# A spectral mixer fused with a SoLU feed-forward block: quarter products gathered behind each pair's seventh product on a new plan, and the exponentials' sum taken to the deviations

## The chip, the core and the metric

The kernel runs on one core of a Trainium2 chip. The metric is device time in microseconds, the median of several executions. Five engines work side by side, each through its own queue in order: TensorE (PE, with its weight loads PEld), VectorE (DVE), ScalarE (ACT), GpSimd (POOL), and SyncE (SP), which only issues DMAs. ACT and POOL issue DMAs too.

## The reference, cut to what matters

```python
# x: 8 entries of 3136 rows x 256 channels
X = np.fft.rfft(x, axis=1)
y = np.fft.irfft(X * (filt_r + 1j * filt_i)[None], n=3136, axis=1)
h = y.reshape(25088, 256) @ w_in                       # 256 x 1024
e = np.exp(h - h.max(-1, keepdims=True))
solu = h * e / (e.sum(-1, keepdims=True) + 1e-9)
mu, var = solu.mean(-1, keepdims=True), solu.var(-1, keepdims=True)
out = ((solu - mu) / np.sqrt(var + 1e-6) * g_ln) @ w_out   # 1024 x 256
```

All of it is float32.

## The kernel before, in words

**Two streams in one queue.** The 25088 rows are 196 blocks of 128, taken in 98 pairs. `step(k)` issues what belongs to block k; even and odd steps of one pair (j = k // 2) differ. Beside this main stream runs the Fourier mixing of the entries still to come: entry 0 and part of entry 1 come first, alone, and entries 2 to 7 are cut into small jobs that are laid between the main stream's products. All is issued in an order written out by hand (`manual_schedule`), so each engine's queue holds its instructions in the order of `step`.

**Main stream of a pair.** The expansion of a pair is a 2x2 by 2x2 block product done with seven products instead of eight (`product(j, m)`, 128x512 each, two instructions): 1, 2, 6, 7 in the even step, 5, 3, 4 in the odd one. Sums of inputs are made by POOL (`pair_sums`). Two PSUM banks take them (`ps_m`); ACT copies bank 0 out (`keep`), DVE adds and takes the running minimum (`finish`). Two blocks later ACT does the exponential with its sum (`exponential`), DVE multiplies (`normalize`, with the sum's inverse as its scalar, made by two DVE instructions on 128x1), a block later DVE transposes 32x32 squares (`turn`), ACT squares for the variance (`square`), and SP regroups the transposed rows by DMA (`regroup`). Once for four blocks POOL makes the deviations (`deviations`) and one small matmul turns them (`regroup_deviations`). The projection is seven products again (`project(p, m)`, 8 instructions of 128x128 each) for a pair p four or five behind: 5, 3, 4 in the even step, 1, 2, 6, 7 in the odd one, in two banks of `ps_o` (bank 0: 1, 6, 5, 3; bank 1: 2, 7, 4). POOL makes the sums (`project_sums`), ACT scales bank 0 out (`keep_out`), DVE scales and adds bank 1 (`finish_out`). Product 4 adds onto bank 1, so it follows the `finish_out(p, 1, 1, ...)` that reads the bank after product 7; the next product 2 starts bank 1 afresh, behind `finish_out(p, 1, 0, ...)`.

**Quarter products.** A job of entries 2 to 7 uses TensorE as four 64x64 arrays. There are four kinds, named by their PSUM tiles:

- `pa`, `first_quarters`: eight in an entry, each after a POOL sum and a DVE difference of the rows; two ACT copies follow, and a store by POOL.
- `pb`, `forward`: seven in an entry; DVE multiplies its result by the filter in two parts of three instructions (`multiply`, `pr` and `pi`).
- `pc`, `inverse`: after both parts; two ACT copies and a store of g follow.
- `py`, `back_halves` with `join_halves`: eight in an entry; one ACT copy and two DVE instructions follow.

`PLAN` gives, for each entry, the steps of the eight `pa`, the seven `pb` and the eight `py`. Lists by step (`early`, `middle`, `late`, `first_parts`, `second_parts`, `loads`, ...) hold the jobs as closures, and `step` empties them at fixed places. PSUM: `ps_t` has two banks in turn (`pa`, `py`), `ps_b` two (`pb`, `pc`), `ps_m` two, `ps_o` two: eight in all.

For an entry from 2 on with a spectrum job at step t, before: `forward` in `early[t]` (middle of an even step), part 0 of `multiply` near the end of the same step, part 1 in the middle of step t + 1, `inverse` at its end. Odd steps open with the finish of product 5, `finish_out(p, 0, 0, ...)`, part 1, `turn`, two `finish`, `normalize` on DVE. A `pa` stands at the end of its step, an odd one for entries 3 to 7; a `py` in the middle of an even one.

Of the kernel before, what the change touches and what calls it, by code (L numbers as in the profile page):

```python
# [17 lines left out]
P = 128  # L18
B, S, C = 8, 3136, 256
DFF = 1024  # L20
# [19 lines left out]
    ([5, 7, 8, 9, 10, 11, 12, 13], range(18, 32, 2), [34, 36, 38, 40, 42, 44, 46, 46]),  # L40
    ([15, 23, 25, 27, 29, 31, 33, 35], range(38, 52, 2), range(54, 70, 2)),
    (range(39, 55, 2), range(58, 72, 2), range(76, 92, 2)),
    (range(63, 79, 2), range(82, 96, 2), range(100, 116, 2)),
    (range(87, 103, 2), range(106, 120, 2), range(126, 142, 2)),
    (range(111, 127, 2), range(130, 144, 2), range(150, 166, 2)),
]
EPS_LN, EPS_SM = 1e-6, 1e-9

# [46 lines left out]
def kernel(  # L95
# [48 lines left out]
    nc.vector.memset(neg_half, -0.5)  # L144

# [45 lines left out]
    class Spectrum:  # L191
# [5 lines left out]
        def __init__(self, e, pools, load, load_de):  # L197
            self.e, self.pools = e, pools
            self.load, self.load_de = load, load_de
            self.spare = {}  # L200
            self.units = [(i, min(2, NP - i)) for i in range(0, NP, 2)]
            self.xs, self.t1s, self.t2s, self.fs, self.prods, self.gs, self.des, self.spectra, self.diffs = (
                {} for _ in range(9))
# [52 lines left out]
        def difference(self, i):  # L256
            rows = slice(0, 64 + N1)
            xi = self.xs[i]
            self.diffs[i] = diff = self.pools["diff"].tile([P, 2, C], FP32, name=f"diff_{self.e}_{i}",
                                                           tag="diff")  # L260
            nc.vector.tensor_tensor(out=diff[rows], in0=xi[rows, 2:4, :], in1=xi[rows, 0:2, :],
                                    op=ALU.subtract)
# [7 lines left out]
        def first_quarters(self, i, pss):  # L270

            xi, diff = self.xs[i], self.diffs.pop(i)
            for j, rhs in enumerate((xi[:, 0:2, :], diff)):
                for g in range(2):
                    rows = (64, NK // 2)[j]
                    nc.tensor.matmul(out=pss[g][64 * j:64 * j + rows],
                                     lhsT=wq_t[64 * g:64 * g + N1, j, 0:rows],
                                     rhs=rhs[64 * g:64 * g + N1], start=True, stop=True)
            rows = slice(0, 64 + NK // 2)
            for g in range(2):  # L280
                nc.scalar.copy(out=xi[rows, 2 * g:2 * g + 2, :], in_=pss[g][rows])
# [359 lines left out]
    def psum_pair(name, other):  # L641
# [11 lines left out]
             for name, bufs in (("r", 4), ("diff", 1), ("t2", 1), ("p", 1), ("g", 1))}  # L653
# [26 lines left out]
    def prepare_w_out(step):  # L680
# [3 lines left out]
        if step == 0:  # L684
# [3 lines left out]
            for i, h, _ in quarters:  # L688
                for f in range(KF // 2):
                    fg = KF // 2 * h + f  # L690
                    nc.vector.tensor_scalar(out=w_out_sb[:, i, f], in0=w_out_sb[:, i, f],
                                            scalar1=g_sb[:, fg:fg + 1], scalar2=-float(DFF),
# [27 lines left out]
    sums, ms, hs, nmaxs, es, solus, squares = {}, {}, {}, {}, {}, {}, {}  # L720
# [61 lines left out]
    def exponential(k):  # L782

        e = wk.tile([P, DFF], FP32, name="e", tag="e")
        esum = small.tile([P, 1], FP32, name="esum", tag="esum", bufs=2)
        nc.scalar.activation(out=e, in_=hs[k], func=AFT.Exp, bias=nmaxs.pop(k)[:, 1:2], scale=-1.0,  # L786
                             accum_out=esum)
        es[k] = e, esum

    def normalize(k):  # L790

        g, i = divmod(k, 4)
        if i == 0:
            variances[g] = small.tile([P, 4], FP32, name=f"var_{g}", tag="var")
        e, esum = es.pop(k)
        rsum = small.tile([P, 1], FP32, name="rsum", tag="rsum", bufs=2)
        nc.vector.tensor_scalar(out=rsum, in0=esum, scalar1=EPS_SM, scalar2=float(DFF), op0=ALU.add,
                                op1=ALU.mult)
        nc.vector.reciprocal(out=rsum, in_=rsum)
        solus[k] = solu = hs.pop(k)  # L800
        nmu = small.tile([P, 1], FP32, name="nmu", tag="nmu", bufs=2)
        nc.vector.scalar_tensor_tensor(out=solu, in0=e, scalar=rsum, in1=solu, op0=ALU.mult,  # L802
# [3 lines left out]
    def square(k):  # L806
# [4 lines left out]
                             accum_out=variances[g][:, i:i + 1])  # L811

# [23 lines left out]

    def deviations(g):
        rs = small.tile([P, 4], FP32, name=f"rs_{g}", tag="rs", bufs=2)
        nc.gpsimd.tensor_scalar(out=rs, in0=variances.pop(g), scalar1=1.0 / DFF, scalar2=EPS_LN,
                                op0=ALU.mult, op1=ALU.add)  # L840
# [67 lines left out]
    def store_out(p):  # L908
# [13 lines left out]
     spectrum_loads) = ([[] for _ in range(blocks + LAG + 1)] for _ in range(11))  # L922

    def ahead(t, by):
        return loads[max(0, t - by)]
# [3 lines left out]
    for e in range(1, B):  # L929
# [5 lines left out]
        for i, t in enumerate(first_at):  # L935
# [10 lines left out]
            else:  # L946

                row_loads.append((t, t - 2, -1, lambda sp=sp, i=i: sp.fetch_quarters(i, nc.sync.dma_start)))
                differences[t].append(lambda sp=sp, i=i: sp.difference(i))
                products[t].append(lambda sp=sp, i=i: sp.sum(i))  # L950
                late[t].append(lambda sp=sp, i=i: sp.first_quarters(
                    i, [psum(f"pa_{sp.e}_{i}_{g}") for g in range(2)]))
                stores[t + 1].append(lambda sp=sp, i=i, dma=dma: sp.store_quarters(i, dma))
        for i, t in enumerate(spectrum_at):
# [5 lines left out]
            fetches = ahead(t, 2) if e == 1 and t < 8 else spectrum_loads[t - 2]  # L960
            fetches.append(lambda sp=sp, i=i, dma=dma: sp.fetch(i, dma))
            ahead(t, 1 if e == 1 and i % 2 == 1 else 2).append(lambda sp=sp, i=i: sp.fetch_filter(i))
            fetches.append(lambda sp=sp, i=i: sp.fetch_de(i))
            early[t].append(lambda sp=sp, i=i, o=other: sp.forward(i, psum_pair(f"pb_{sp.e}_{i}", o)))
# [9 lines left out]
        for ch, t in enumerate(back_at):  # L974
            row_loads.append((
                t, t - 1, spectrum_at[-1] + 2, lambda e=e, ch=ch: fetch_back(e, ch)))
# [16 lines left out]

    def step(k):
# [5 lines left out]
        sums_of_x = differences[k] + products[k]  # L1000
# [22 lines left out]
        if not odd:  # L1023
# [35 lines left out]
            for job in spectrum_loads[k]:  # L1059
                job()  # L1060
# [23 lines left out]
            for job in second_parts[k] + middle[k] + first_parts[k]:  # L1084
                job()
            if proj and p not in last:
                finish_out(p, 1, 0, (1, 0), 1)
                store_out(p)
        else:
# [77 lines left out]
```

## Time and profile before

| | |
|---|---|
| median of 3 runs | 1602.72 us (1601.0 to 1605.67) |
| profiled execution, span from first to last instruction | 1598.0 us |
| mean granted TensorE clock in it | 0.997 |
| PE / DVE / ACT / POOL busy | 1548.0 / 1310.2 / 915.8 / 1177.0 us |
| idle before ACT L901, ended by PE | 244.6 us |
| HBM read, written | 124.51 MB, 81.40 MB |

The span is the profiled execution's own time; what lies around it is not seen in the profile. Pair 9 begins at 245.1 us, pair 97 at 1546.0 us. A line `L754` is `product`, `L885` is `project`, `L308` a `forward` or `inverse`, `L276` `first_quarters`, `L381` `back_halves`, `L802` `normalize`, `L818` `turn`, `L775` and `L778` `finish`, `L905` `finish_out`, `L329` to `L331` `multiply`, `L261` `difference`. In a timeline the first two columns are the start and the time of a run of like instructions, both in us; in the table of groups the figures are count, busy us, mean ns of one, and idle us of the engine before them.

### The profile page before, as it was taken

The numbers are of one execution on the slowest core, as the hardware profiler recorded it, in microseconds if no ns is written. First come the engines' busy times: TensorE is split into PE (matmuls) and PEld (weight loads), VectorE is DVE, ScalarE is ACT, GpSimd is POOL, SyncE is SP. The second block draws the span as 40 slices with busy tenths as digits, with TensorE's granted clock in tenths as the row PEclk, the third lists the DMA queues.
The fourth block names the chain that finished last, engine by engine and source line by source line (L and its number), as shares of the span: only waits on it lengthen the run. The fifth ranks groups of instructions, "written<-read, shape, count | busy, mean of one in ns | idle before, by whom it ended". The sixth has DMA issues, their size and how long they took to land. (4 is left out here: it accounts for less than half of the span.)

```text
span 1598.0 us, 37061 instructions
## 1 busy us (share of the span) xinstructions
PE 1548.0 (97%) x12828; PEld 1055.5 (66%) x12828; DVE 1310.2 (82%) x2639; ACT 915.8 (57%) x1825; POOL 1177.0 (74%) x1371
## 2 busy tenths in 40 slices
PE   5998999999999999999999999999999999999997
PEld 1463567666666676667766776667776777777777
DVE  1887888998998889888988889987898777777773
ACT  2245655656565656565566656665555666665653
POOL 4555986688768867886778877886866867677775
PEclk8999999999999999999999999999999999999999
DMA  9989978776987588766886678766784544343434
GB/s 261 288 272 261 262 214 236 215 228 175 247 245 231 157 230 238 230 177 169 235 240 195 166 196 256 209 183 174 222 220 127 134 125 127 96 113 99 113 103 115
DMA packets 343804, 311.14 MB, mean 195 GB/s; under 512 B 27835, under 2 KB 310100, under 8 KB 343620
## 3 DMA queue, kind: packets, MB, share of 16 engines
q1 hardware_dynamic: 271476, 170.45, 40.4%
q0 software_dynamic: 33744, 98.81, 20.6%
q10 hardware_dynamic: 38400, 39.53, 8.2%
q8 instruction: 104, 1.70, 0.5%
q14 instruction: 80, 0.65, 0.1%
HBM read 124.51 MB, written 81.40 MB: 129 GB/s over the span
## 5 line engine op out<-in xcount | busy, mean ns | idle before, releaser
L885 PEld LDWEIGHTS o<-w_out_sb,solu_t 128*128 128x128 f32 x3136 | 381.5, 192 | 50.2 <-issue 43.2
L885 PE MATMUL o<-w_out_sb,solu_t 128*128 128x128 f32 x3136 | 401.5, 276 | 3.8 <-DVE ot L905 3.1
L754 PE MATMUL m<-w_in_sb,s 128*128 128x512 f32 x784 | 397.9, 608 | 2.1 <-ACT h L764 1.4
L885 PEld LDWEIGHTS o<-w_out_sb,u 128*128 128x128 f32 x2352 | 305.9, 191 | 140.7 <-issue 104.0
L802 DVE SCALAR_TENSOR_TENSOR h<-e,rsum,h 128x1024 f32<-128x1024 f32 x196 | 321.2, 1639 | 6.9
L885 PE MATMUL o<-w_out_sb,u 128*128 128x128 f32 x2352 | 310.4, 275 | 3.0 <-POOL u L733 2.1
L754 PE MATMUL m<-w_in_sb,y 128*128 128x512 f32 x588 | 306.6, 604 | 3.0 <-DVE h L775 2.1
L764 ACT COPY h<-m 128x512 f32<-128x512 f32 x294 | 173.2, 589 | 201.8 <-PE m L754 193.6
L901 ACT ACTIVATE ot<-o,rs_t 128x128 f32<-128x128 f32 x392 | 143.2, 366 | 248.0 <-PE o L885 244.6
L733 POOL TENSOR_TENSOR u<-solu_t 128x512 f32<-128x512 f32 x98 | 133.5, 1362 | 178.3 <-DMA solu_t<-turn 157.0
L810 ACT ACTIVATE h<-h,nmu 128x1024 f32<-128x1024 f32 x196 | 224.6, 1146 | 47.0 <-DVE turn L818 37.4
L818 DVE STREAM_TRANSPOSE turn<-h 128x1024 f32<-128x1024 f32 x196 | 243.1, 1241 | 3.1
L778 DVE CUSTOM_DVE_ANT_0 h<-m,h 128x512 f32<-128x512 f32 x196 | 133.2, 679 | 131.6 <-ACT h L764 94.5
L786 ACT ACTIVATE e<-h,nmax 128x1024 f32<-128x1024 f32 x196 | 225.1, 1148 | 20.1 <-DVE h L802 18.8
L733 POOL TENSOR_TENSOR u<-solu_t,u 128x512 f32<-128x512 f32 x98 | 147.6, 1506 | 94.0 <-PE o L885 94.0
L754 PEld LDWEIGHTS m<-w_in_sb,s 128*128 128x128 f32 x784 | 127.9, 190 | 88.0 <-issue 68.3
L905 DVE SCALAR_TENSOR_TENSOR ot<-o,rs_t,ot 128x128 f32<-128x128 f32 x299 | 103.7, 347 | 73.8 <-ACT ot L901 55.6
L733 POOL TENSOR_TENSOR u<-u,solu_t 128x512 f32<-128x512 f32 x98 | 152.0, 1551 | 15.2 <-PE o L885 7.2
L733 POOL TENSOR_TENSOR solu_t<-solu_t,solu_t 128x512 f32<-128x512 f32 x98 | 161.8, 1651 | 0.9
L754 PEld LDWEIGHTS m<-w_in_sb,y 128*128 128x128 f32 x588 | 96.3, 190 | 98.1 <-issue 54.7
L733 POOL TENSOR_TENSOR s<-y 128x128 f32<-128x128 f32 x196 | 97.9, 500 | 0.5
L381 PEld LDWEIGHTS py<-wb_t,t 50*64 50x64 f32 x3584 | 57.6, 134 | 42.9 <-issue 22.5
(126 smaller groups left out, 2001.6 us busy)
## 6 DMA issues: line engine op xcount, KB each, us to landing
solu_t<-turn SPq DMA_DIRECT2D x780, 128.0 KB
out_dram<-ot SPq DMA_DIRECT2D x196, 128.0 KB
t<-d POOLq DMA_DIRECT2D x112, 200.0 KB, 6.8
d<-x POOLq DMA_DIRECT2D x100, 200.0 KB, 5.0
f<-f_dram POOLq DMA_DIRECT2D x39, 512.0 KB, 8.2
t<-d ACTq DMA_DIRECT2D x37, 512.0 KB
d<-g POOLq DMA_DIRECT2D x36, 512.0 KB, 4.9
x<-in_x_dram SPq DMA_DIRECT2D x112, 98.0 KB
```

What stands on the lines that cost most here:

```text
L381: nc.tensor.matmul(out=views[g][64 * h:64 * h + 64, cb, i, :], lhsT=t4[rows, i, c0:c0 + 64], rhs=wb_t[rows, 0:N1], start=True, stop=True)
L733: nc.gpsimd.tensor_tensor(out=out, in0=in0, in1=in1, op=op)
L754: nc.tensor.matmul(out=ms[j, bank], lhsT=lhsT, rhs=w_in_sb[:, w, :], start=m in (1, 2, 7), stop=True, skip_group_check=True)
L764: nc.scalar.copy(out=h_half(k, i), in_=ms[j, 0])
L778: nc.vector.tensor_tensor_reduce(out=h_half(k, i), in0=ms[j, bank], in1=h_half(*kept), scale=1.0, scalar=sofar, op0=ALU.add, op1=ALU.min, ...
L786: nc.scalar.activation(out=e, in_=hs[k], func=AFT.Exp, bias=nmaxs.pop(k)[:, 1:2], scale=-1.0, accum_out=esum)
L802: nc.vector.scalar_tensor_tensor(out=solu, in0=e, scalar=rsum, in1=solu, op0=ALU.mult, op1=ALU.mult, accum_out=nmu)
L810: nc.scalar.activation(out=solu, in_=solu, func=AFT.Square, bias=nmu, scale=-float(DFF), accum_out=variances[g][:, i:i + 1])
L818: nc.vector.transpose(out=turns[g][:, :, i, :], in_=solus[k].rearrange("p (f j) -> p f j", j=32))
L885: nc.tensor.matmul(out=pos[p, bank], lhsT=lhs[:, f, :], rhs=w[:, f, :], start=f == 0 and (m in (1, 2, 7) or alone), stop=True, skip_group_ ...
L901: nc.scalar.activation(out=out_half(p, *to)[0], in_=pos[p, 0], func=AFT.Copy, scale=rs)
L905: nc.vector.scalar_tensor_tensor(out=ot, in0=pos[p, bank], scalar=rs, in1=out_half(p, *kept)[0], op0=ALU.mult, op1=ALU.add)
```

## The change

1. **Places of the jobs.** For entries 2 to 7, `forward`, `inverse`, `back_halves` (and `first_quarters` of entries 3 to 7) go into a list `gathered[t]`. A new function `gather` runs them one behind the other at the end of an even step, behind the pair's seventh product of the step's list (product 7), each with two PSUM banks of its own: 0 is `ps_t`, 1 `ps_b`, 2 `ps_o`, in this order. `multiply` part 0 goes from step t to the end of t + 1, part 1 from the middle of t + 1 to the end of t + 2, `inverse` from t + 1 to t + 2, the store of g one step later.
2. **Plan.** `first_at` and `back_at` of entries 2 to 7 are new, so that the three kinds that meet in a step fit the three places.
3. **Fetches of the spectrum** (two DMAs on ACT's queue) go from the middle of an even step to its end.
4. **Sums and differences.** `difference` is made in place, as 2b - (a + b), from POOL's sum; the sum stands one step earlier, and the `diff` pool goes.
5. **Exponentials' sum.** `normalize` multiplies by a constant; the sum is kept for four blocks, squared on ACT (`least_variance`) with the epsilon's root, and added to the variance in `deviations`, whose square root it scales. The constant of `w_out` follows.
6. **Order.** `finish_out(p, 1, 0, ...)` and the store go ahead of the multiplies at the end of an even step.

The diff, cut to its core:

```diff
-    ([5, 7, 8, 9, 10, 11, 12, 13], range(18, 32, 2), [34, 36, 38, 40, 42, 44, 46, 46]),
-    ([15, 23, 25, 27, 29, 31, 33, 35], range(38, 52, 2), range(54, 70, 2)),
-    (range(39, 55, 2), range(58, 72, 2), range(76, 92, 2)),
-    (range(63, 79, 2), range(82, 96, 2), range(100, 116, 2)),
-    (range(87, 103, 2), range(106, 120, 2), range(126, 142, 2)),
-    (range(111, 127, 2), range(130, 144, 2), range(150, 166, 2)),
+    ([5, 7, 8, 9, 10, 11, 12, 13], range(18, 32, 2), [34, 36, 36, 38, 40, 42, 44, 46]),
+    (range(18, 34, 2), range(38, 52, 2), range(56, 72, 2)),
+    ([48, 50, 52, 52, 54, 54, 56, 58], range(62, 76, 2), range(80, 96, 2)),
+    ([72, 74, 76, 76, 78, 78, 80, 82], range(86, 100, 2), range(104, 120, 2)),
+    ([96, 98, 100, 100, 102, 102, 104, 106], range(110, 124, 2), range(128, 144, 2)),
+    ([120, 122, 124, 124, 126, 126, 128, 130], range(134, 148, 2), range(152, 168, 2)),
...
+SHRINK = 1.0 / (32 * DFF)
...
         def difference(self, i):
...
-            nc.vector.tensor_tensor(out=diff[rows], in0=xi[rows, 2:4, :], in1=xi[rows, 0:2, :],
-                                    op=ALU.subtract)
+            nc.vector.scalar_tensor_tensor(out=xi[rows, 2:4, :], in0=xi[rows, 2:4, :], scalar=2.0,
+                                           in1=xi[rows, 0:2, :], op0=ALU.mult, op1=ALU.subtract)
...
     def normalize(k):
...
-        nc.vector.tensor_scalar(out=rsum, in0=esum, scalar1=EPS_SM, scalar2=float(DFF), op0=ALU.add,
-                                op1=ALU.mult)
-        nc.vector.reciprocal(out=rsum, in_=rsum)
...
-        nc.vector.scalar_tensor_tensor(out=solu, in0=e, scalar=rsum, in1=solu, op0=ALU.mult,
+        nc.vector.scalar_tensor_tensor(out=solu, in0=e, scalar=SHRINK, in1=solu, op0=ALU.mult,
                                        op1=ALU.mult, accum_out=nmu)
...
+    def least_variance(g):
+        floors[g] = floor = small.tile([P, 4], FP32, name=f"floor_{g}", tag="floor")
+        nc.scalar.activation(out=floor, in_=esums.pop(g), func=AFT.Square, bias=floor_sb,
+                             scale=EPS_LN ** 0.5)
...
     def deviations(g):
-        nc.gpsimd.tensor_scalar(out=rs, in0=variances.pop(g), scalar1=1.0 / DFF, scalar2=EPS_LN,
-                                op0=ALU.mult, op1=ALU.add)
+        nc.gpsimd.tensor_tensor(out=rs, in0=variances.pop(g), in1=floors.pop(g), op=ALU.add)
...
+                    products[t - 1].append(lambda sp=sp, i=i: sp.sum(i))
+                    differences[t].append(lambda sp=sp, i=i: sp.difference(i))
+                    gathered[t].append((None, f"pa_{sp.e}_{i}", sp.first_quarters, i))
...
-            fetches = ahead(t, 2) if e == 1 and t < 8 else spectrum_loads[t - 2]
+            fetches = ahead(t, 2)
...
+            if e > 1:
+                gathered[t].append((1, f"pb_{sp.e}_{i}", sp.forward, i))
+                first_parts[t + 1].append(lambda sp=sp, i=i: sp.multiply(i, 0))
+                second_parts[t + 2].append(lambda sp=sp, i=i: sp.multiply(i, 1))
+                gathered[t + 2].append((2, f"pc_{sp.e}_{i}", sp.inverse, i))
+                stores[t + 3].append(lambda sp=sp, i=i: sp.store(i, nc.gpsimd.dma_start))
+                continue
...
+            if e > 1:
+                gathered[t].append((0, f"py_{e}_{ch}", lambda ch, pss, e=e: (
+                    back_halves(e, ch, pss), join_halves(e, ch)), ch))
+                continue
...
+    def gather(jobs):
+        wanted = {home for home, *_ in jobs}
+        spare = [home for home in range(3) if home not in wanted]
+        placed, used = [], set()
+        for home, name, run, i in jobs:
+            if home is None or home in used:
+                home = spare.pop(0)
+            used.add(home)
+            placed.append((home, name, run, i))
+        for home, name, run, i in sorted(placed, key=lambda job: job[0]):
+            run(i, [psum(f"{name}_{u}") for u in range(2)] if home == 0 else psum_pair(name, home == 2))
...
             if 2 <= k < blocks + 2:
                 normalize(k - 2)
-            for job in second_parts[k] + middle[k] + first_parts[k]:
-                job()
             if proj and p not in last:
                 finish_out(p, 1, 0, (1, 0), 1)
                 store_out(p)
+            for job in second_parts[k] + middle[k] + first_parts[k]:
+                job()
+            gather(gathered[k])
```

## The prediction

> **What bounds the kernel now.** I read the page first (busy shares, then the costliest groups), then TensorE's timeline around the small jobs, then VectorE's timeline in the same kind of pair, and last the start of each pair's first product through the whole span.
>
> ```profile
> span 1598.0 us, 37061 instructions
> PE 1548.0 (97%) x12828; PEld 1055.5 (66%) x12828; DVE 1310.2 (82%) x2639; ACT 915.8 (57%) x1825; POOL 1177.0 (74%) x1371
> ...
> L802 DVE SCALAR_TENSOR_TENSOR h<-e,rsum,h 128x1024 f32<-128x1024 f32 x196 | 321.2, 1639 | 6.9
> ```
>
> TensorE (PE) is busy for 97% of the span and VectorE (DVE) for 82%. Only what shortens PE's stream or its waits can gain; DVE is close behind. From product 1 of one pair to product 1 of the next, a pair without quarter jobs takes 12.26 us (12.48 where the little `o<-turn_t` matmul is in it). That is 14 products at 0.86 (expansion, P) or 0.89 us (projection, O), so PE is the bound there with nothing between.
>
> ```profile
> 1102.84 1.02 PE L754 MATMUL m<-w_in_sb,y 128*128 128x512 f32 x2
> 1103.79 1.15 PE L381 MATMUL py<-wb_t,t 50*64 50x49 f32 x64
> 1104.87 1.12 PE L754 MATMUL m<-w_in_sb,s 128*128 128x512 f32 x2
> 1105.84 1.05 PE L885 MATMUL o<-w_out_sb,u 128*128 128x128 f32 x8
> ...
> 1116.60 1.02 PE L754 MATMUL m<-w_in_sb,y 128*128 128x512 f32 x2
> 1117.56 1.15 PE L381 MATMUL py<-wb_t,t 50*64 50x49 f32 x64
> 1118.53 1.11 PE L308 MATMUL pb<-t,de 64*64 64x256 f32 x16
> 1119.56 1.13 PE L754 MATMUL m<-w_in_sb,s 128*128 128x512 f32 x2
> 1120.52 1.05 PE L885 MATMUL o<-w_out_sb,u 128*128 128x128 f32 x8
> ```
>
> Starts tell the price of a job. From 1102.84 to 1105.84 there are 3.00 us with two products (1.72) in them, so a `py` alone costs 1.28. From 1116.60 to 1120.52 there are 3.92, so `py` and `pb` side by side cost 2.20. A `pc` alone cost 1.24 (1128.42 to 1131.41, less 0.89 and 0.86). Side by side saves about 0.35: the product before a group starts 0.09 early, the two after it 0.26 late. Work without that is 0.93 for `py` and 0.86 for `pa`, `pb`, `pc`. With 12.26 or 12.48, these prices and 0.36 a group, I get every pair from 9 to 96 within a few hundredths, except some with several jobs; the excess over those 88 pairs is 20 us in all (19 of it in pairs 9 to 72), and 3 us in pairs 5 to 8.
>
> ```profile
> 809.11 0.35 DVE L905 SCALAR_TENSOR_TENSOR ot<-o,rs_t,ot 128x128 f32<-128x128 f32 x1 [0.52 <-ACT ot L901]
> ...
> 810.69 0.69 DVE L331 TENSOR_TENSOR pi<-pi,pt 128x512 f32<-128x512 f32 x1
> 811.30 1.24 DVE L818 STREAM_TRANSPOSE turn<-h 128x1024 f32<-128x1024 f32 x1
> 812.46 0.71 DVE L775 TENSOR_SCALAR_CACHE_REDUCE h<-m,nmax 128x512 f32<-128x512 f32 x1
> ...
> 813.10 0.75 DVE L778 CUSTOM_DVE_ANT_0 h<-m,h,nmax 128x512 f32<-128x512 f32 x1
> ...
> 813.77 0.15 DVE L797 TENSOR_SCALAR rsum<-esum 128x1 f32<-128x1 f32 x1
> 813.96 0.16 DVE L799 RECIPROCAL rsum<-rsum 128x1 f32<-128x1 f32 x1
> 814.15 1.28 DVE L802 SCALAR_TENSOR_TENSOR h<-e,rsum,h 128x1024 f32<-128x1024 f32 x1
> ```
>
> This is the odd step of a full pair. DVE runs without a gap from 809.11 on, because the second multiply of the quarter spectrum (`pi`) stands between the `ot` that waits for project(p, 2) and the transpose. Start to start: `ot` 0.26, transpose 1.16, the two finishes 0.64 and 0.67, `rsum` chain 0.38, normalize 1.21 to 1.33.
>
> **Part by part, against the span.** *Groups.* By the plans, entries 2 to 7 make 121 groups before (one of them in pair 7) and 79 after; the work is the same. 42 x 0.35 = -15.
>
> *Exponentials' sum.* Two DVE instructions and their dependences go, 0.37 x 196 = 72 us of DVE. Off PE's path this is worth nothing by itself; I credit it in the waits below, -3 for the excess of pairs 5 to 8 and -1 for the last normalizes, which stand in the closing chain. The 49 new ACT squares of 128x4 (nearest row: the 128x4 copy, 0.16) are 8 us on an engine that waits 244.6 us for PE at L901 alone: 0, up to +8 uncovered. The POOL add in place of a tensor_scalar lies between 0.36 (that row) and 1.07 (the pow beside it); its result is used in a later pair: 0.
>
> *Differences.* In place, behind POOL's sum instead of ahead of it: 0.68 of DVE at least, as `diff` now (L261; mean 0.946). But all now open an even step, ahead of transpose, finish and the `ot` that project(p, 4) waits for; entries 3 to 7 had them in odd steps.
>
> *DMA issues.* The spectrum's two fetches leave the middle of an even step and stand on ACT behind the group's evacuations, ahead of the copy of product 5. ACT then has 2 copies (1.07 start to start), 2 issues (0.37 each) and the copy (0.59) = 2.40 from the group's end; product 3, which needs that copy done, comes 0.26 + 3 products = 2.9 later. Covered by 0.5; without cover up to 0.6 in 40 pairs, 24 us. On POOL the stores of g wait for those copies, and sums and pair sums stand behind the stores: 1.1 + 0.79 + 2 x 0.53 + 1.28 + 4 x 0.5 = 6.2 after the group, product 6 is due at 9. Where two `pa` share a group it is 8.6: nearly late.
>
> The Trainium skill's "TensorEngine Tiling (Array Packing)", PSUM Bottleneck, speaks against the grouping here: packed tiles speed up TensorE and not the evacuation, which may become the bottleneck; by it the 24 us would be added.
>
> *The new wait.* All multiplies of entries 2 to 7 move a step later, part 0 to the end of an odd step, part 1 to the end of the next even one. In the odd step DVE now has nothing while the group runs (the first finish waits for product 5 behind it), and from the `ot` behind project(p, 2) to the `ot` that frees the bank for project(p, 4) its queue is, by start-to-start spacings: 0.26 + 1.16 + 0.64 + 0.67 + normalize 1.21 + part 0 (0.60 + 0.71 + 0.65) + difference 0.61 + transpose 1.16 + finish 0.62 + `ot` 0.26 = 8.55, and 0.3 for handing over at both ends: 8.85. PE has 3, 4, O6, O7, 1, O5, 2, 6, O3 in between: 5 x 0.86 + 4 x 0.89 = 7.86. So 1.0 us of PE stalls where the difference is there (`pa`), 0.4 without.
>
> On top comes what DVE's two-operand instructions lose beside POOL. The rows show it: normalize 1.28 at least, 1.639 on average; the `pr` add 0.72 and 1.007; the difference 0.68 and 0.946. That is 0.35 + 0.29 + 0.26 in this chain. Today such losses fall mostly into slack. Then, from that `ot` to `pb` behind the group's first job, DVE needs 1.21 + 0.26 + 2 x 0.60 = 2.7 and PE has 2.75, so normalize's 0.35 is stalled there too. A pair with `pa`, `pb`, `pc` waits 2.25, one with `py`, `pb`, `pc` 1.4.
>
> The Trainium skill's "SBUF — State Buffer", Who interferes with whom, says the loser blocks until the other's instruction ends; by it each loss could reach a POOL sum, 1.28, instead of the mean I take.
>
> By the plan, pairs 9 on: 14 of the first kind x 2.25 = 31; 20 of the second x 1.4 = 28; 4 with a half-size unit and two differences, about 2.0 each, and one of 1.1 = 9; the two pairs with `pb` and `pc` but no job ahead of `pb`, 2.3 each, and the pair after them 1 = 6; 12 with `pa` and no multiply, 0.5 each for POOL's lateness = 6. Sum +80. The 19 us of waits seen in pairs 9 to 72 go with the old order: -19 (they come back if POOL's long blocks hit as they do now).
>
> Sum: -15 - 3 - 1 - 19 + 80 = +42, span 1640. The runs' median, 1602.7, is 4.7 above the profiled span, so 1645. Ends: with no losses to POOL the waits are 14 x 1.0 + 20 x 0.4 + 7 = 29, which gives -9, 1594; with each loss in the 34 full pairs twice what I took (+42), 1687.
>
> **Rivals.** (1) Faster. The stalls don't arise, because POOL now idles until the group's copies are done and DVE's lost time shrinks while its queue has 0.37 less per normalize. With no new wait all that is left is -15 - 3 - 1 - 19: 1565; with half the structural ones about 1580. The point that decides: 38 us over some 39 full pairs, so below 1.0 us of stall a pair it is faster. For it: DVE runs 15 us of work in 16.6 us pairs today and PE hardly waits. Against: 8.85 against 7.86 needs no contention at all.
> (2) Slower still. POOL becomes the loop: its stores wait for the group's copies, so pair sums come late to product 6, and u's crowd against normalize, adds and differences. 2 us in each of the 34 full pairs more than mine: about 1690 and above. For it: POOL is 74% busy, and 6.2 of 9 us are taken without contention.
> (3) No difference: 15 + 23 us of gains meet some 38 of stalls.
>
> **Numbers.** Forecast 0.55, rival (1) 0.27, rival (2) 0.14, (3) 0.04. About 0.3% (5 us) is what a measurement of this kernel can tell from no change. Rivals (2) and the forecast are slower: 0.69. The range runs from 1578, inside the faster case, to 1690; the forecast alone is 1610 to 1685.
>
> **What would show it.** Right: pairs with three jobs at 16.5 to 18 us instead of 15.3; idle PE before `o` at L885 released by the `ot` of DVE, and before `pb`, `pc` by the multiplies; DVE waiting about 3 us a pair for product 5's copy; groups of jobs whose neighbours start 0.09 and 0.26 late once a pair. Wrong: three-job pairs near 15.3 us, or PE's waits ended by POOL's pair sums.

## The result and the profile after

The changed kernel takes 1724.5 us (median of 4 runs, 1722.2 to 1726.2) beside 1604.2 us for the kernel before: 1.077 times as long (95% interval 1.074 to 1.080). The sign was forecast, the size was not: 80 us above the 1645, and outside the range. Of the four runs of diff2_own, below, one lay 1.6% above the fastest and is left out, in its time and its interval.

The profiled execution spans 1720.4 us, 4 us under the median. From the page after (line numbers of the changed kernel: L893 `project`, L757 `product`, L803 `normalize`, L781 and L778 `finish`, L913 `finish_out`, L332 to L334 `multiply`, L264 `difference`, L270 POOL's sum of rows):

```profile
span 1720.4 us, 36762 instructions
PE 1583.3 (92%) x12828; PEld 1081.6 (63%) x12828; DVE 1241.4 (72%) x2248; ACT 927.0 (54%) x1874; POOL 1196.0 (70%) x1371
...
PE 54%; DMA 17%; DVE 16%; issue 5%; POOL 3%; SPq 3%; ACT 1%; DVEq 0%; POOLq 0%; ACTq 0%
...
L893 PE MATMUL o<-w_out_sb,solu_t 128*128 128x128 f32 x3136 | 410.0, 280 | 63.1 <-DVE ot L913 60.6
...
L803 DVE SCALAR_TENSOR_TENSOR h<-e,h 128x1024 f32<-128x1024 f32 x196 | 303.2, 1547 | 0.1
L781 DVE CUSTOM_DVE_ANT_0 h<-m,h 128x512 f32<-128x512 f32 x196 | 132.7, 677 | 216.9 <-ACT h L767 193.2
```

VectorE (DVE) lost 69 us of work, and TensorE (PE) is busy for 92% instead of 97%. In the chain that ended last DMAs now have 17% of the span and DVE 16% (1% each before, where the chain could be followed over only a quarter of the span). PE now waits 60.6 us before `o` for `finish_out`, and DVE waits 193.2 us in front of product 5's `finish`, against 94.5 before. Its queue is idle there and late a little further on. One full pair on PE (the last columns: what the idle time before waited for):

```profile
895.06 1.02 PE L757 MATMUL m<-w_in_sb,y 128*128 128x512 f32 x2
895.92 1.05 PE L893 MATMUL o<-w_out_sb,u 128*128 128x128 f32 x8
896.82 1.02 PE L757 MATMUL m<-w_in_sb,y 128*128 128x512 f32 x2
897.68 1.02 PE L757 MATMUL m<-w_in_sb,s 128*128 128x512 f32 x2
898.53 1.05 PE L893 MATMUL o<-w_out_sb,u 128*128 128x128 f32 x8
901.28 1.16 PE L893 MATMUL o<-w_out_sb,solu_t 128*128 128x128 f32 x8 [1.70 <-DVE ot L913]
902.28 1.02 PE L757 MATMUL m<-w_in_sb,s 128*128 128x512 f32 x2
903.23 1.15 PE L384 MATMUL py<-wb_t,t 50*64 50x49 f32 x64
904.20 1.11 PE L311 MATMUL pb<-t,de 64*64 64x256 f32 x16
```

The stall is at product 4 of the projection, where the prediction put it; `py`, `pb`, `pc` follow product 7 as one group.

PE is also busy for 35 us more (1583.3 against 1548.0) with the same 12828 instructions. Behind some of the longer stalls the trace shows a granted clock of 0.5. Pairs 12 and 14, with the same jobs, stall for 2.10 and 2.15 us before product 4. The figures are the stretch, its length, then busy time and instructions of PE, PEld, DVE, ACT and POOL, the mean granted clock, the share of the DMA engines and GB/s:

```profile
348.35:367.90 19.55, 17.45 (x115) 12.12 (x113) 14.14 (x25) 9.98 (x21) 12.29 (x14) 0.91 0.70 195
387.27:405.24 17.97, 15.82 (x114) 10.95 (x113) 14.19 (x25) 9.98 (x21) 12.14 (x14) 1.00 0.75 211
```

Seven of the pairs 12 to 74 have such a stretch of 3.4 us, 23.9 us in all, and pairs 9 to 11 have 20.5 us; the kernel before has none between 41 and 1597 us.

The span cut by pairs (start of a pair's product 1 on PE), with the kernels tried below; all in us:

| | to pair 0 | pairs 0-8 | 9-11 | 12-74 | 75-96 | rest | span |
|---|---|---|---|---|---|---|---|
| before | 97.0 | 148.1 | 54.0 | 963.3 | 283.7 | 52.0 | 1598.0 |
| after | 106.5 | 163.3 | 78.6 | 1032.9 | 282.9 | 56.3 | 1720.4 |
| before_shift32 | 107.8 | 154.2 | 55.0 | 989.1 | 284.0 | 55.0 | 1645.1 |
| sum_256 | 96.0 | 151.8 | 54.3 | 959.0 | 282.5 | 52.2 | 1595.8 |
| after_256 | 95.2 | 161.6 | 75.0 | 1036.7 | 282.9 | 52.0 | 1703.4 |
| part0_256 | 96.3 | 159.7 | 81.4 | 962.7 | 282.7 | 52.0 | 1634.8 |
| best2_256 | 96.5 | 151.9 | 52.6 | 975.0 | 282.6 | 53.0 | 1611.6 |

Of the 122.4 us, 69.6 lie in pairs 12 to 74, 24.6 in 9 to 11, 15.2 in 0 to 8, and 13.8 before pair 0 and behind pair 96, where the change alters next to nothing.

### The profile page after: what moved, and what is told of

Same layout as the page of the kernel before. It is cut to its first block, busy times and chain, and to the rows that moved or that the text cites. A ratio compares the mean times of both kernels' runs of the same rounds, so it can differ in the third digit from the quotient of the medians.

```text
span 1720.4 us, 36762 instructions
## 1 busy us (share of the span) xinstructions
PE 1583.3 (92%) x12828; PEld 1081.6 (63%) x12828; DVE 1241.4 (72%) x2248; ACT 927.0 (54%) x1874; POOL 1196.0 (70%) x1371
## 3 DMA queue, kind: packets, MB, share of 16 engines
q1 hardware_dynamic: 271476, 170.45, 43.7%
## 4 chain that ended last, share of the span: by engine, by line
PE 54%; DMA 17%; DVE 16%; issue 5%; POOL 3%; SPq 3%; ACT 1%; DVEq 0%; POOLq 0%; ACTq 0%
PE o L893 23%; PE m L757 21%; DMA x<-in_x_dram 5%; DMA solu_t<-turn 5%; DVE turn L821 4%; DVE h L803 3%; DVE h L781 3%; PE py L384 3%; DMA d<-x 2%; PE pa L279 2%; DMA t<-d 2%; PE pc L311 2%; PE pb L311 2%; SPq L838 2%; POOL u L736 1%
## 5 line engine op out<-in xcount | busy, mean ns | idle before, releaser
L893 PE MATMUL o<-w_out_sb,solu_t 128*128 128x128 f32 x3136 | 410.0, 280 | 63.1 <-DVE ot L913 60.6
L893 PEld LDWEIGHTS o<-w_out_sb,solu_t 128*128 128x128 f32 x3136 | 385.7, 194 | 118.5 <-DVE ot L913 69.6
L757 PE MATMUL m<-w_in_sb,s 128*128 128x512 f32 x784 | 421.9, 625 | 8.9 <-POOL s L736 7.1
L893 PEld LDWEIGHTS o<-w_out_sb,u 128*128 128x128 f32 x2352 | 309.3, 194 | 142.3 <-issue 91.2
L893 PE MATMUL o<-w_out_sb,u 128*128 128x128 f32 x2352 | 313.9, 277 | 3.9 <-POOL u L736 3.2
L757 PE MATMUL m<-w_in_sb,y 128*128 128x512 f32 x588 | 301.2, 595 | 8.1 <-DVE nmax L781 6.2
L803 DVE SCALAR_TENSOR_TENSOR h<-e,h 128x1024 f32<-128x1024 f32 x196 | 303.2, 1547 | 0.1
L781 DVE CUSTOM_DVE_ANT_0 h<-m,h 128x512 f32<-128x512 f32 x196 | 132.7, 677 | 216.9 <-ACT h L767 193.2
L757 PEld LDWEIGHTS m<-w_in_sb,s 128*128 128x128 f32 x784 | 129.2, 194 | 104.9 <-issue 67.9
L736 POOL TENSOR_TENSOR u<-solu_t,u 128x512 f32<-128x512 f32 x98 | 139.5, 1424 | 69.3 <-PE o L893 69.3
L913 DVE SCALAR_TENSOR_TENSOR ot<-o,rs_t,ot 128x128 f32<-128x128 f32 x299 | 103.9, 348 | 107.6 <-ACT ot L909 53.8
L736 POOL TENSOR_TENSOR u<-u,solu_t 128x512 f32<-128x512 f32 x98 | 165.9, 1692 | 15.9 <-PE o L893 5.4
L736 POOL TENSOR_TENSOR solu_t<-solu_t,solu_t 128x512 f32<-128x512 f32 x98 | 155.8, 1590 | 0.0
L757 PEld LDWEIGHTS m<-w_in_sb,y 128*128 128x128 f32 x588 | 96.8, 191 | 63.9 <-issue 40.6
L736 POOL TENSOR_TENSOR s<-y 128x128 f32<-128x128 f32 x196 | 116.0, 592 | 0.7
L353 POOL DMA_DIRECT2D d<-g x42 | 32.4, 772 | 108.4 <-ACT g L349 102.6
```

Source lines behind the costliest of these rows:

```text
L736: nc.gpsimd.tensor_tensor(out=out, in0=in0, in1=in1, op=op)
L757: nc.tensor.matmul(out=ms[j, bank], lhsT=lhsT, rhs=w_in_sb[:, w, :], start=m in (1, 2, 7), stop=True, skip_group_check=True)
L781: nc.vector.tensor_tensor_reduce(out=h_half(k, i), in0=ms[j, bank], in1=h_half(*kept), scale=1.0, scalar=sofar, op0=ALU.add, op1=ALU.min, ...
L803: nc.vector.scalar_tensor_tensor(out=solu, in0=e, scalar=SHRINK, in1=solu, op0=ALU.mult, op1=ALU.mult, accum_out=nmu)
L893: nc.tensor.matmul(out=pos[p, bank], lhsT=lhs[:, f, :], rhs=w[:, f, :], start=f == 0 and (m in (1, 2, 7) or alone), stop=True, skip_group_ ...
L913: nc.vector.scalar_tensor_tensor(out=ot, in0=pos[p, bank], scalar=rs, in1=out_half(p, *kept)[0], op0=ALU.mult, op1=ALU.add)
```

## The experiments

Theory at first: the wait that part 0 of `multiply` makes, as forecast but larger, and late rows at the start. The rivals stand in the expectations. Times are medians; each has the kernel before beside it on the same chip (1599 to 1604 us).

**The wait.** part0_early:

```diff
-                first_parts[t + 1].append(lambda sp=sp, i=i: sp.multiply(i, 0))
+                odd_first[t + 1].append(lambda sp=sp, i=i: sp.multiply(i, 0))
...
         else:
+            for job in odd_first[k]:
+                job()
             if hid and k >= LAG:
                 product(j, 5)
```

> The changed kernel with one move: part 0 of multiply (entries 2 to 7) stands at the start of the odd step, ahead of the finish of product 5, instead of at its end. Theory: the three DVE instructions of part 0 (1.96 us) lie in the chain to the finish_out that project(p, 4) waits for, and DVE idles about 3 us ahead of the finish of product 5. Then the stall before project(p, 4) goes in pairs with py, pb, pc (1.77 us each, 20 pairs) and shrinks from 3.6 to about 1.5 in those with pa, pb, pc (12): 50 to 60 us less than the changed kernel, about 1668. Rival: the stall is what DVE loses beside POOL, which stays wherever part 0 stands: at most 15 us less, about 1710.

1652.8 us, 1.034 (1.030 to 1.039): 72 us less for three DVE instructions moved into the time in which DVE waited for product 5, more than the 50 to 60 expected. The same was run later with the tiles in place (part0_256, below), and two kernels then differ in this alone. PE's waits in after_256, and in part0_256:

```profile
PE o L893 <- DVE ot L913: 61.9, 47, 3.0
```

```profile
PE o L893 <- DVE ot L913: 4.0, 10, 1.0
```

And DVE's queue in the same pair, first after_256:

```profile
876.52 1.65 DVE L803 SCALAR_TENSOR_TENSOR h<-e,h 128x1024 f32<-128x1024 f32 x1
...
878.10 0.68 DVE L332 TENSOR_TENSOR pr<-pb,f 128x512 f32<-128x512 f32 x1
878.70 0.68 DVE L333 TENSOR_TENSOR pt<-pb,f 128x512 f32<-128x512 f32 x1
879.41 1.67 DVE L334 TENSOR_TENSOR pr<-pr,pt 128x512 f32<-128x512 f32 x1
881.00 1.23 DVE L821 STREAM_TRANSPOSE turn<-h 128x1024 f32<-128x1024 f32 x1
882.16 0.65 DVE L781 CUSTOM_DVE_ANT_0 h<-m,h 128x512 f32<-128x512 f32 x1
...
882.75 0.34 DVE L913 SCALAR_TENSOR_TENSOR ot<-o,rs_t,ot 128x128 f32<-128x128 f32 x1
...
889.78 0.69 DVE L781 CUSTOM_DVE_ANT_0 h<-m,h 128x512 f32<-128x512 f32 x1 [1.96 <-ACT h L767]
```

then part0_256:

```profile
840.82 1.65 DVE L803 SCALAR_TENSOR_TENSOR h<-e,h 128x1024 f32<-128x1024 f32 x1
...
842.52 1.25 DVE L821 STREAM_TRANSPOSE turn<-h 128x1024 f32<-128x1024 f32 x1
844.14 0.69 DVE L781 CUSTOM_DVE_ANT_0 h<-m,h 128x512 f32<-128x512 f32 x1 [0.38 <-ACT e L791]
...
844.76 0.35 DVE L913 SCALAR_TENSOR_TENSOR ot<-o,rs_t,ot 128x128 f32<-128x128 f32 x1
```

The normalize ahead takes 1.65 us in both. In the first, 2.90 us of part 0 (its add 1.67, against 0.69 where nothing disturbs it) stand between it and the transpose, and the `ot` that frees the bank starts 6.23 us after the normalize instead of 3.94. The pair takes 17.34 us, without part 0 there 15.37. In the first, DVE then stands idle for 1.96 us in front of product 5's `finish`: the work had a place that cost nothing. Without the stalls no stretch at half the clock is left in pairs 12 to 74, and PE is busy there for 953.4 us instead of 971.2: 18 of the 74 us that these pairs gain.

**The start.** plan3_late moves entry 3's first jobs:

```diff
-    (range(18, 34, 2), range(38, 52, 2), range(56, 72, 2)),
+    ([22, 24, 26, 28, 30, 32, 32, 34], range(38, 52, 2), range(56, 72, 2)),
```

> The changed kernel with entry 3's first products at steps 22, 24, 26, 28, 30, 32, 32, 34 instead of 18 to 32. Theory: pairs 10 and 11 (33.9 and 27.1 us, 25 above PE's work) are long because entry 3's rows share four row tiles with entry 1's last eight chunks (steps 16 to 22), so that their fetches start late; with the rows apart the pairs take under 21 us and the time falls by 15 to 25 us, about 1704. Rival: the fetches are late because SP's queue holds them behind regroups that wait for a late transpose; then pairs 10 and 11 stay over 24 us and the time within 8 us of 1724.

1711.2 us, 1.071 (1.063 to 1.079). Pair 10 fell from 33.9 to 22.7 us, pair 11 only from 27.1 to 26.8.

diff2_own gives entry 2's differences a tile of their own again, ahead of the sum:

```diff
         def difference(self, i):
...
+            if self.e == 2:
+                self.diffs[i] = diff = self.pools["diff"].tile([P, 2, C], FP32, ...)
+                nc.vector.tensor_tensor(out=diff[rows], in0=xi[rows, 2:4, :], in1=xi[rows, 0:2, :],
+                                        op=ALU.subtract)
+                return
...
-                    products[t].append(lambda sp=sp, i=i: sp.sum(i))
-                    differences[t].append(lambda sp=sp, i=i: sp.difference(i))
+                    products[t].append(lambda sp=sp, i=i: sp.difference(i))
+                    differences[t].append(lambda sp=sp, i=i: sp.sum(i))
```

> The changed kernel, but entry 2 has its differences in a tile of their own again, issued on DVE ahead of POOL's sum. Theory: in pairs 2 to 6 DVE now waits for POOL's sum (15.1 us in 4 waits between 142 and 225 us) and all behind it waits; that goes, so pairs 2 to 6 shrink by 12 to 18 us, about 1709. Rival: the longer start is DMA time of the rows, which the difference only shows: within 4 us of 1724.

1710.3 us, 1.071 (1.065 to 1.077), 14 less; the interval overlaps with the changed kernel's, so by itself this is not settled. sum_behind puts the sums of the odd steps behind the pair sums:

```diff
-        for job in top[k] + (sums_of_x + stores[k] if k < LAG else stores[k] + sums_of_x):
+        for job in top[k] + (sums_of_x if k < LAG else []) + stores[k]:
             job()
...
             pair_sums(j + 1)
+        for job in sums_of_x if k >= LAG else []:
+            job()
```

> The changed kernel, but GpSimd's sums of entries 3 to 7 stand behind the pair sums of y in their odd step instead of ahead of them, so product 6 no longer waits behind a row fetch. Theory: product 6 waited 4.6 us for the pair sums in pairs 9 to 11 (L757 after POOL s), because GpSimd stood at a sum whose rows came 10.4 us late; that goes, pairs 10 and 11 lose 5 to 10 us together: 1710 to 1718 us. Rival: the late rows stop the same pair at the difference or at pa instead: 1720 to 1728 us.

1756.8 us, 1.097 (1.093 to 1.101): both wrong, 32 us slower. PE's wait for `ot` grew from 60.6 to 94.2 us. POOL in pair 10 of the changed kernel shows why the sum matters so much:

```profile
283.31 1.05 POOL L368 DMA_DIRECT2D t<-d  x2
284.36 1.02 POOL L290 DMA_DIRECT2D d<-x  x2
295.74 1.26 POOL L270 TENSOR_TENSOR x<-x 113x512 f32<-113x512 f32 x1 [10.36 <-DMA x<-in_x_dram]
296.96 0.45 POOL L736 TENSOR_TENSOR s<-y 128x128 f32<-128x128 f32 x1
```

The sum now runs a step earlier, its fetch does not. POOL stands at it, the pair sums behind it are late for product 6 (4.6 us of PE in pairs 9 to 11), and the difference, at the head of DVE's queue, waits as well. In sum_behind the sum is later still, and by the longer wait for `ot` DVE pays for it. No run puts the sum back into its own step, so the earlier sum and the new plan's use of the four row tiles are not told apart.

**The sum part.** sum_only is the kernel before with the exponentials' sum alone (part 5 of the change). It was expected to confirm a small gain:

> The kernel before with one part of the change alone: the exponentials' sum kept for the deviations, normalize with a constant. Theory: 72 us of DVE go, all but some of it beside PE's work; the excess of 20 us over PE's own work in pairs 9 to 96 falls by about half and the closing chain by 1: 1604 becomes 1588 to 1600. Rival: DVE's load is no part of the excess (long blocks by POOL make it): 1604 within 3 us.

1629.8 us, 1.019 (1.015 to 1.024): slower by 31 us. Neither theory had this. In one of its pairs an add took 2.77 us that took 0.94 before, so the next theory was DVE's phase against POOL. sum_pad keeps the two small instructions in front of each `normalize`, their result unread:

```diff
+        nc.vector.tensor_scalar(out=rsum, in0=esums[g][:, i:i + 1], scalar1=EPS_SM, scalar2=float(DFF),
+                                op0=ALU.add, op1=ALU.mult)
+        nc.vector.reciprocal(out=rsum, in_=rsum)
         nc.vector.scalar_tensor_tensor(out=solu, in0=e, scalar=SHRINK, in1=solu, op0=ALU.mult,
```

> The kernel before with the exponentials' sum part alone, and VectorE still runs the two small instructions on the exponentials' sum ahead of each normalize, though nothing reads their result. Theory (phase): the part alone was 31 us slower because VectorE, 0.37 us earlier at each normalize, meets GpSimd's sums at other places (an add of 2.77 us beside one, against 0.94); with VectorE as late as before the time is 1598 to 1612 us. Rival (the squares of 128x4 on ScalarE, the floors and the new dependences): 1622 to 1636 us.

1647.8 us, 1.028 (1.023 to 1.032): 18 us more, not less. But `rsum` also takes room again, 64 bytes of each partition, and so moves every tile behind it once more, which turned out to matter below; this run doesn't settle the phase theory. gather_only is the changed kernel with part 5 of the change undone:

> The changed kernel with the exponentials' sum as before: VectorE makes rsum (two instructions of 0.15 and 0.16 us) ahead of each normalize again, and the two ScalarE squares of 128x4 and the floors are gone. Theory: what the sum part cost in the kernel before (+31 us when it was added alone) does not depend on the order of the jobs, so taking it out gives about that back: 1690 to 1700 us, and pair 9 starts some 10 us earlier. Rival: the new order waits on VectorE's queue, so 0.37 us more in front of each normalize is paid at the PSUM bank of project(p, 4) in some 34 pairs with three jobs: 1735 to 1745 us.

1746.3 us, 1.090 (1.087 to 1.094): the rival was right, `rsum` costs in the new order. But its pair 0 began at 97.7 us, where the changed kernel's began at 106.5, and combo2's at 97.0. combo2 has part0_early, plan3_late, sum_behind and no sum part:

> The changed kernel with four steps of it altered at once: part 0 of the multiply at the start of the odd step (-72 us alone), entry 3's first jobs from step 22 (-13 alone), sums behind the pair sums, and the exponentials' sum as before. Theory (the losses lie in different pairs and add): 1724 - 72 - 13 - 10 - 27 = 1602 us, 1595 to 1612. Rival (they hide one another, since the start waits for rows whatever is moved): 1625 to 1640 us.

1690.0 us, 1.059 (1.053 to 1.065); neither. All three kernels without the sum part began pair 0 at 97.0 to 97.7, the others at 98.8 to 109.1, though nothing of the sum part runs before pair 0 but one memset. What differs is where tiles lie. Two lines of the change, left out of the core above:

```diff
+    floor_sb = consts.tile([P, 1], FP32, name="floor_sb")
+    nc.vector.memset(floor_sb, EPS_LN ** 0.5 * EPS_SM)
```

stand ahead of `y`. By the program's allocation the tile takes 32 bytes of each partition, and the small tiles of four columns 128 more, so every large tile begins elsewhere.

**The place of the tiles.** before_shift32 is the kernel before with nothing but an unused tile there:

```diff
+    floor_sb = consts.tile([P, 1], FP32, name="floor_sb")
+    nc.vector.memset(floor_sb, 0.5)
```

> The kernel before with nothing changed but one unused tile of one column (32 bytes) allocated ahead of y and set once. Theory (place of the tiles): 1630 to 1655 us, pair 0 later than 98 us. Rival: 1597 to 1607 us.

1647.2 us, 1.029 (1.026 to 1.033): 47 us for a tile that nothing reads. after_align, sum_align and part0_align made the tile 64 bytes (`[P, 16]`), so that large tiles begin on multiples of 64:

> The changed kernel with the one-column tile floor_sb allocated 16 columns wide. As changed, that tile takes 32 bytes of each partition ahead of y, so y and every large tile behind it (rows, spectra, solu_t, h) begins 32 bytes off a multiple of 64; with 64 bytes they begin on a multiple again, as before. Nothing else differs. Theory (place of the tiles): all kernels with the misplaced tiles began pair 0 at 98.8 to 109.1 us, the three without them at 97.0 to 97.7; transfers to and from misplaced tiles are slower, which costs the prologue 9 us and makes rows late through the whole kernel: pair 0 at 97 to 98 us and 1665 to 1700 us in all. Rival (the squares, floors and dependences of the sum part cost it, and the start varies by chance): 1718 to 1730 us.

1729.2 us, 1.079 (1.076 to 1.083).

> The kernel before with the exponentials' sum part alone, and floor_sb 16 columns wide, so that the tiles behind it stay on multiples of 64 bytes. Theory (place of the tiles): the part's own effect is what keeping the two small instructions cost (1648 - 1630 = 18 us), so 1580 to 1600 us, not above the kernel before. Rival (squares, floors, dependences): 1622 to 1636 us, as with the one-column tile.

1632.7 us, 1.022 (1.017 to 1.026).

> The changed kernel with part 0 of the multiply at the start of the odd step, and floor_sb 16 columns wide. Theory (place of the tiles): 1653 less what the misplaced tiles cost, 30 to 50 us: 1600 to 1625 us. Rival: 1647 to 1660 us.

1655.9 us, 1.035 (1.031 to 1.039). No change in any: not multiples of 64. So either the place was not the cause of the rest, or 64 was the wrong multiple. Queue q1 decided, whose packets and bytes are the same in all kernels. The kernel before, before_shift32, sum_align:

```profile
q1 hardware_dynamic: 271476, 170.45, 40.4%
```

```profile
q1 hardware_dynamic: 271476, 170.45, 43.4%
```

```profile
q1 hardware_dynamic: 271476, 170.45, 47.4%
```

The last column is a share of 16 engines' span: 0.404 x 16 x 1598.0 = 10330 engine-us, then 11420 and 12320. By where `y` and the large tiles behind the small ones begin, in bytes past a multiple of 256: before 0 and 0, before_shift32 32 and 32, changed kernel 32 and 160 (12030), sum_align 64 and 192, sum_pad 32 and 224 (12610, the most of all). The engines' own instructions kept their times: in before_shift32 the normalize took 1.640 us on average and the transpose 1.240, against 1.639 and 1.241. So the last six kernels were built with `floor_sb` taken from the small pool behind `y` and the total growth brought to 512 bytes:

```diff
-    floor_sb = consts.tile([P, 1], FP32, name="floor_sb")
+    floor_sb = small.tile([P, 96], FP32, name="floor_sb", tag="floor_sb", bufs=1)
```

> The kernel before with the exponentials' sum part alone, but floor_sb taken from the small pool behind y and widened to 384 bytes, so that y begins where it did and every large tile behind the small ones begins 512 bytes later, on a multiple of 512 as in the kernel before. Theory (multiple of 256): the transfers of queue q1 take 10200 to 10400 engine-us again (12300 with the tiles 160 or 192 bytes off), pair 0 starts at 97 to 98 us, and the part by itself is at worst neutral: 1580 to 1605 us. Rival (the place was not it, or not all of it; squares, floors, dependences): 1622 to 1636 us.

1595.4 us, 0.995 (0.993 to 0.997): the sum part alone, with its tiles in place, is faster than the kernel before, and the only version here that beats both. q1 took 10340 engine-us. 31 us of loss became 8 of gain by the place of a constant. DVE is 0.37 us earlier at each normalize here too, so the phase theory falls with this run.

> The changed kernel with floor_sb placed in the same way, so that its large tiles begin on multiples of 512 bytes. Theory (multiple of 256): 1724 less the 30 to 50 us that the place cost: 1675 to 1695 us, pair 0 at 97 to 98 us; what is left over the kernel before is the wait of the new order and the start. Rival: 1718 to 1732 us.

1705.5 us, 1.063 (1.060 to 1.067), 19 less than the changed kernel. Below the expected 30 to 50: pairs 12 to 74 gained nothing (1036.7 against 1032.9), so there, it seems, slower transfers were hidden by the waits that the order makes anyway (argued, not shown). The gain is before pair 0 (11.3) and behind pair 96 (4.3). after_256 and gather_only both have tiles in place: `rsum` costs 41 us in the new order, 8 in the old.

part0_256 adds the edit of part0_early:

> The changed kernel with part 0 of the multiply at the start of the odd step, and the tiles on multiples of 512 bytes. Theory (the two losses add): 1653 - 30 to 50 = 1603 to 1623 us. Rival (with rows in time the wait for part 0 would have been smaller too, or the start waits all the same): 1630 to 1650 us.

1630.0 us, 1.016 (1.013 to 1.018): part 0's place is worth 75 us. That is the rival's lower end; the two losses don't simply add.

best_256 adds those of plan3_late and diff2_own:

> As part0_256, with entry 3's first jobs from step 22 on and entry 2's differences in a tile of their own ahead of GpSimd's sum. Theory (with rows in time these two work as their single tests of 13 and 9 us, and more since no row is late behind them): 1575 to 1600 us, faster than the kernel before. Rival: they hide each other or part0_256's gain, 1605 to 1625 us.

1618.1 us, 1.008 (1.005 to 1.012): in the rival's range. Pairs 4 and 5 fell from 47.7 to 39.7 us (36.6 before), pair 10 from 34.3 to 19.9, pair 11 only from 29.5 to 26.7.

best2_256 moves entry 3's first jobs once more:

```diff
-    ([22, 24, 26, 28, 30, 32, 32, 34], range(38, 52, 2), range(56, 72, 2)),
+    ([24, 26, 28, 30, 32, 32, 34, 34], range(38, 52, 2), range(56, 72, 2)),
```

> As best_256, but entry 3's first jobs stand in steps 24, 26, 28, 30, 32, 32, 34, 34 instead of 22, 24, 26, 28, 30, 32, 32, 34, so that none runs beside entry 1's last jobs, which hold the row buffers. Theory (a sum a step earlier stops GpSimd until its row lands): pair 11, 26.7 us with 11.6 us of GpSimd waiting for a row and 3.2 us of product 6 behind it, falls to 16 to 18 us and the whole to 1604 to 1612 us. Rival (the SyncE queue brings any row of that time late): the same loss moves to pair 12 or 13, 1615 to 1622 us.

1611.8 us, 1.006 (1.002 to 1.009). Pairs 9 to 11 are down to 52.6 us, below the kernel before, so late rows were their whole loss. But pair 17 now takes 26.9 us instead of 14.6, and the waits in it are the same as in pair 10 above:

```profile
POOL x L276 <- DMA x<-in_x_dram: 10.9, 1, 10.9
...
PE m L763 <- POOL s L742: 9.5, 1, 9.5
```

Theory and rival both held a part: the row that is one step late has moved.

best3_256 moves the differences of entries 3 to 7 as well:

```diff
-                    differences[t].append(lambda sp=sp, i=i: sp.difference(i))
+                    late_differences[t].append(lambda sp=sp, i=i: sp.difference(i))
...
                 finish_out(p, 1, 1, (0, 1), 1)
-            for job in early[k]:
+            for job in late_differences[k] + early[k]:
```

> As best2_256, with the differences of entries 3 to 7 behind the second finish_out of the even step instead of at its head. Theory (what is left in pairs with first jobs, 0.6 to 1.4 us in some 25 pairs, is the difference of 0.7 to 1.0 us ahead of transpose, finish and finish_out): 10 to 18 us less than best2_256. Rival (that excess is the pa jobs' own, or GpSimd's lateness): within 4 us of best2_256.

1632.7 us, 1.017 (1.012 to 1.022), 21 slower than best2_256 and against both. PE waits 13.0 us before `pa` and 11.4 before `pb` for the second part of `multiply`: with the difference behind `finish_out`, part 1 comes late to the group.

## Why the prediction missed

**Right.** That the change would be slower, and by which wait. PE stalls before product 4 of the projection on DVE's `finish_out`, because part 0 of `multiply` went into DVE's full stretch while it idles behind the group; moving that one step back took 72 and 75 us away. Product 5's copy holds DVE 193.2 us. Over pairs 12 to 74 there are 40 groups fewer, 14 us at the prediction's own price. The small classes hold: twelve pairs with `pa` and no multiply 5.9 us (6 forecast), the last three 6.7 (6 with their neighbour, 2.3 each and 1), the half-size pairs with two differences 8.7 (9). The copies behind a group did not become the limit: for ACT, PE waited 1.7 us before the expansion's products and 1.6 before `o`. Not seen was the second wait, the 0.35 before `pb`: PE waited 0.5 us there in all. At the upper end of the sum, doubling the losses of the 34 full pairs makes 14 x 1.25 + 20 x 0.99 = 37 and not 42, so 1682 and not 1687.

**The stalls, mis-sized.** 20 pairs with `py`, `pb`, `pc` lose 1.77 us each over PE's own work, not 1.4 (+7 us). 12 of the 14 pairs with `pa` lose 3.6 each, not 2.25 (+16 us); after_256 has the same sums within 6 us. DVE's instructions lost more there than the means that were taken: the add took 1.21 us on average in the 20 pairs and 1.07 in the 12, not 1.007, and the difference in the 12 took 1.48, not 0.946. In the pair shown the normalize takes 1.65 us, as its mean before (1.639), but part 0's add 1.67. The mean was the wrong size for instructions that moved to another place beside POOL. The Trainium skill's "SBUF — State Buffer", Who interferes with whom, was weighed for this, that the loser blocks to the other's end, as a bound of 1.28 us a loss. The add here lost 0.98, above the 0.29 taken; in sum_only one lost 2.08 (2.77 against 0.69), so a single POOL sum of 1.28 was no bound either. The clock behind a stall was no term of the sum at all: 23.9 us at 0.5 in pairs 12 to 74 are, as an estimate, 12 us of PE's work, about half of the 23.

**The start, the step that failed.** "Differences ... 0.68 of DVE at least, as `diff` now" gave this part no cost in time, and the moved sum none at all: only the spectrum's fetches and the stores were followed through the queues, not the row fetch that the sum waits for. Measured with the tiles in place: 13.5 us in pairs 0 to 8, of which entry 2's own tile returned 8 in pairs 4 and 5 (the rest was not traced), and 21.0 in pairs 9 to 11, which best2_256 took away there, though 12 came back in pair 17.

**The place of the tiles, not in the prediction at all.** A constant of one column and a few small tiles were read as arithmetic, not as an allocation. That is 19 us of the changed kernel's time, and 47 in the kernel before.

By the spans, 1720.4 against the 1640 of the sum, the 80 us are: 17 the place (the changed kernel against after_256), and then, in after_256, 16.5 the start (13.5, and 3 credited for pairs 5 to 8), 17.5 the late rows of pairs 10 and 11 (22.0 over PE's work, less the 4.5 that the two stalls forecast in them), 26 the size of the stalls, and 3 in small terms. The measured time is where rival (2) put it, 1690 and above, but not for its reason: GpSimd as the loop is seen only in single pairs where it stands at a row, and before `m` PE waits 7.1 us for its sums in all.

## What to carry to other kernels

Work that is put off in a queue should go to where that queue is seen waiting, not to where it is next convenient: the same three instructions cost 75 us in one place and next to nothing in the other. A stall can cost more than its idle time, so compare the busy time of the same instructions and the granted clock behind it too. When an operation is moved earlier, follow what feeds it, its fetch included, or the queue stands at it. And treat any new SBUF tile, however small, as a change of every address behind it: compare the transfers' own time for the same packets before explaining a slower kernel by its instructions.

## What the runs showed of the hardware

Where tiles begin changes the time of the same transfers: 271476 packets and 170.45 MB took 10100 to 10340 engine-us in the kernels with tiles 0 bytes past a multiple of 256, 11420 with 32, 11970 to 12060 with 160, 12280 to 12330 with 192. One unused 32-byte tile cost 47 us of 1601 that way, 10.8 of them before pair 0 and 25.8 in pairs 12 to 74. The Trainium skill's "DMA: Bandwidth & Descriptors", How a descriptor splits into AXI transactions, says that a descriptor that doesn't start 256-byte-aligned fetches from the boundary below and pays for the unused bytes. As an estimate from that page, a 512-byte piece takes 16 beats in place, 17 when 32 bytes past the boundary, 21 when 160 and 22 when 192 past: 6, 31 and 38% more. The queue's 200320 packets of 512 bytes took 32.8 ns each on average in the kernel before, 37.4 in before_shift32, 40.9 in the changed kernel and 42.0 in sum_align: 14, 25 and 28% more. The runs agree in direction and order, with more for 32 bytes than the estimate and less for the others. No run here tells 128 from 256 or 512: all the fast kernels have the tiles behind the small ones on multiples of 512, and `y` on 256.

The granted clock can fall behind a stall. In pairs 12 to 74 of the changed kernel PE stalled 13 times for 1.8 us or more; behind seven of these the clock was 0.5 for 3.4 us, beginning within 1.5 us of the stall's end, and behind the other six and all shorter ones it stayed at 1. What decides between two stalls of 2.1 us is not shown.
